# Hand order for the first stage, more staging tiles and a reordered finish in a gated MLP with a spectral branch

## Chip, cores, metric

The kernel runs on one core of a Trainium2 chip. The metric is device time in microseconds (us) of one execution; a median over several executions is given. The record sorts executions into a fast and a slow state by their time; every execution whose state is on record is fast but one of the kernel before (581.7 us, in group 4 of the experiments), which is left out of the ratios. Ratios are of one kernel's fast runs to the other's in the same rounds on the same chip, so they are not quite the ratios of the medians quoted. The kernel before had medians between 572.7 and 577.7 us in the different rounds, so differences of a per cent are judged within rounds.

## The reference

`x` is 2048 rows of 576 numbers (S = 2048, D = 576), bf16. It is normalised over its rows (LN1). One branch filters it in the frequency domain; the other is a gated MLP with a mixing over rows; silu of the second multiplies the first.

```python
xn = _layernorm(x)                                   # LN1
# branch A: spectral filter
X  = rfft2(xn);  X = X * (w_r + 1j*w_i);  s = irfft2(X)
# branch B: gated MLP
z  = gelu(xn @ w_in)                                 # 576 -> 2 * 2304
z1, z2 = z[..., :2304], layernorm(z[..., 2304:])
g  = w_sp @ z2 + b_sp[:, None]                       # 2048 x 2048 mixing of rows
b  = (z1 * g) @ w_out                                # 2304 -> 576
out = x + s * silu(b)
```

## The kernel before

All DFTs are matmuls by constant matrices. The stages on TensorE, in the names that the kernel uses, are:

- `xpose` and `p0`: for each of 16 row tiles of 128 rows, normalise, transpose (5 matmuls) and do the DFT over D (10 matmuls). The result is copied to a staging tile and stored to DRAM (`Ad`).
- `p1`: read `Ad` back by columns, first half of the DFT over S. `p2`, `p3`: second half, product with the filter, and back. `p4`, `p5`: inverse, stored to DRAM as `Yd`.
- `z2`: units of 5 matmuls (0.81 us) that make the second half of `z`. They have no part in the spectral chain, so `fill(n)` puts n of them into TensorE's program where it would otherwise wait.
- main stage: `z1`, the mixing `pg` and the last product `po`, with `p4` and `p5` in between. `outm` finishes a row tile.

The SyncE and TensorE programs are in the order of the source (`manual_schedule`); the other engines are ordered by a scheduler.

```python
    STG = [reg("STG", i * 2 * L, 2 * L) for i in range(3)]          # three staging tiles
    ...
    def p0(m):
        pa = psa.tile([P, 2, 512], F32, tag="a")
        ...                                                          # 10 matmuls
        sg = STG[m % 3].rearrange("p (c l) -> p c l", c=2)
        nc.scalar.activation(out=sg, in_=pa[:, :, 0:L], func=ACT.Identity)
        nc.gpsimd.dma_start(out=Adw[m], in_=sg)
    ...
    def p2(hh):
        ...
        for c in range(2):
            nc.vector.tensor_tensor(out=tt[:, c, :, :], in0=pa[:, :, 0:L], in1=wt[:, c, hh % 4:hh % 4 + 2, :], op=ALU.mult)
    ...
    def outm(q, i):
        m = 4 * q + i
        b = m % 2
        nc.sync.dma_start(out=XIN[b], in_=xv[:, m, :])
        nc.sync.dma_start(out=YIN[b], in_=Yd[m * P:(m + 1) * P, :])
        po = psa.tile([P, 2, 512], F32, tag="a")                     # psa has two buffers
        ...                                                          # 36 matmuls
        nc.scalar.activation(out=th, in_=po[:, :, 0:H2], func=ACT.Tanh, scale=0.5)
        nc.vector.scalar_tensor_tensor(out=g, in0=th, scalar=1.0, in1=po[:, :, 0:H2], op0=ALU.add, op1=ALU.mult)
        nc.vector.tensor_tensor(out=GO[b], in0=GO[b], in1=YIN[b], op=ALU.mult)
        nc.vector.tensor_tensor(out=GO[b], in0=GO[b], in1=XIN[b], op=ALU.add)
        nc.sync.dma_start(out=out2[m * P:(m + 1) * P, :], in_=GO[b])
    ...
            if fi == 0 and q > 0:                                    # four tiles finished at a time
                for i in range(4):
                    outm(q - 1, i)
                if q + 1 < NQ:
                    load_slab(q + 1)                                 # four transposing loads of w_sp
```

All loads, all stores of `outm` and the loads of w_in for the next stage go through the one SyncE queue, in the order of the source.

Of the kernel before, what the change touches and what calls it, by code (L numbers as in the profile page):

```python
# [15 lines left out]
P = 128  # L16
# [64 lines left out]
def kernel(  # L81
# [55 lines left out]
    TH = pers.tile([P, 2, D], F32)  # L137
    make_identity(nc, ident[:])
    eps = pers.tile([P, 1], F32)
# [12 lines left out]
    def reg(name, off, n):  # L152
        return AR[:, offs[name] + off: offs[name] + off + n]
# [11 lines left out]
    XN = [reg("XN", i * KS * P, KS * P) for i in range(3)]  # L165
    STG = [reg("STG", i * 2 * L, 2 * L) for i in range(3)]
    AIN = [reg("AIN", i * 8 * L, 8 * L) for i in range(4)]
    TT = [reg("TT", i * 4 * L, 4 * L).rearrange("p (c h l) -> p c h l", c=2, h=2) for i in range(2)]
# [10 lines left out]
    U = [RW[:, i * 512:(i + 1) * 512] for i in range(NU)]  # L179

    for i in range(3):
        nc.gpsimd.memset(XN[i][:, D:KS * P], 0.0)

    def load_x(c):
        t = AIN[c][:, 0:4 * D].rearrange("p (m d) -> p m d", m=4)
        if c == 0:
            for i in range(4):
                nc.sync.dma_start(out=t[:, i, :], in_=xv[:, i, :])
        else:
            nc.sync.dma_start(out=t, in_=xv[:, 4 * c:4 * c + 4, :])  # L190
        return t

    wv = B_w_in[0:(KS - 1) * P, :].rearrange("(k p) f -> p k f", p=P)
    XC = [load_x(0), load_x(1)]
    nc.sync.dma_start(out=CDSD, in_=cd_cdsd.ap().rearrange("p (k c l) -> p k c l", k=KS, c=2))
    XC += [load_x(2), load_x(3)]
    nc.gpsimd.memset(WIN2[KT:P, KS - 1, :], 0.0)
# [14 lines left out]
    def ln1(ms):  # L212
        n = len(ms)
        mv = small.tile([P, n, 2], F32, tag=f"mv{n}", bufs=3)
        for i, m in enumerate(ms):
            st = small.tile([P, 2, 6], F32, tag="st1", bufs=4)
            for h in range(2):
                nc.vector.bn_stats(out=st[:, h, :], in_=XC[m // 4][:, m % 4, h * H2:(h + 1) * H2])
            nc.vector.bn_aggr(out=mv[:, i, :], in_=st[:])
        if ms[0] < 4:  # L220
            rs = small.tile([P, n], F32, tag=f"rs{n}", bufs=3)
            nc.scalar.activation(out=rs[:], in_=mv[:, :, 1], func=ACT.Sqrt, bias=eps[:], scale=1.0)
            nc.vector.reciprocal(out=rs[:], in_=rs[:])
        else:
            rs = rstd_of(mv, n, f"l1{n}")
        for i, m in enumerate(ms):
            ln1_of[m] = (mv[:, i, 0:1], rs[:, i:i + 1])
# [15 lines left out]
    def p0(m):  # L243
        pa = psa.tile([P, 2, 512], F32, tag="a")
        for ks in range(KS):
            for c in range(2):
                nc.tensor.matmul(pa[:, c, 0:L], lhsT=xnT[:, m, ks, :], rhs=CDSD[:, ks, c, :],  # L247
                                 start=(ks == 0), stop=(ks == KS - 1))
        sg = STG[m % 3].rearrange("p (c l) -> p c l", c=2)
        nc.scalar.activation(out=sg, in_=pa[:, :, 0:L], func=ACT.Identity)  # L250
        nc.gpsimd.dma_start(out=Adw[m], in_=sg)
# [31 lines left out]
    def p2(hh):  # L283
        ain = AIN[(hh // 8) ^ 2].rearrange("p (h l) -> p h l", h=8)
        wt = WCH[(hh // 4) % 2]
        tt = TT[(hh // 2) % 2]
        pa = psa.tile([P, 2, 512], F32, tag="a")
        for j in range(2):
            nc.tensor.matmul(pa[:, j, 0:L], lhsT=MM[:, 0, :], rhs=ain[:, hh % 8 + j, :], start=True, stop=True)
        for c in range(2):  # L290
            nc.vector.tensor_tensor(out=tt[:, c, :, :], in0=pa[:, :, 0:L], in1=wt[:, c, hh % 4:hh % 4 + 2, :], op=ALU.mult)  # L291
        if hh % 4 == 2 and hh // 4 + 2 < 8:
            load_w(hh // 4 + 2)
# [49 lines left out]

    z2s = {}

    def z2(u):
        m, n = u // NZC, u % NZC
        on_act = m % 2 == 1 and m < MT - 2
        if n == 0:
# [10 lines left out]
        else:  # L360
            nc.scalar.activation(out=zc, in_=ph[:], func=ACT.Gelu_apprx_tanh)  # L361
            nc.vector.bn_stats(out=st[:, n, :], in_=zc)
        if n < NZC - 1:
            return
        mv = small.tile([P, 1, 2], F32, tag="mvz")
# [48 lines left out]
    def outm(q, i):  # L414
# [4 lines left out]
        po = psa.tile([P, 2, 512], F32, tag="a")  # L419
        for fi in range(FT):  # L420
            for h in range(2):
                nc.tensor.matmul(po[:, h, 0:H2], lhsT=U[(q * FT + fi) % NU][:, i * P:(i + 1) * P],  # L422
                                 rhs=WOUT[:, fi, h * H2:(h + 1) * H2], start=(fi == 0), stop=(fi == FT - 1))
        th = TH[:, b, :].rearrange("p (h d) -> p h d", h=2)
        g = GO[b].rearrange("p (h d) -> p h d", h=2)
        nc.scalar.activation(out=th, in_=po[:, :, 0:H2], func=ACT.Tanh, scale=0.5)  # L426
        nc.vector.scalar_tensor_tensor(out=g, in0=th, scalar=1.0, in1=po[:, :, 0:H2], op0=ALU.add, op1=ALU.mult)  # L427
        nc.vector.tensor_tensor(out=GO[b], in0=GO[b], in1=YIN[b], op=ALU.mult)
        nc.vector.tensor_tensor(out=GO[b], in0=GO[b], in1=XIN[b], op=ALU.add)
        nc.sync.dma_start(out=out2[m * P:(m + 1) * P, :], in_=GO[b])  # L430

# [8 lines left out]

    def fill(n):
        for u in zq:
            z2(u)
            n -= 1
            if n == 0:
                break

    with tc.manual_schedule(engines={mybir.EngineType.SP, mybir.EngineType.PE}):
        groups = [[0], [1], [2, 3], [4, 5, 6, 7], [8, 9, 10, 11], [12, 13, 14, 15]]
        nc.sync.dma_start(out=MM, in_=cd_mm.ap().rearrange("p (a k) -> p a k", a=3))  # L450
        load_w(0)
        load_w(1)
        nc.sync.dma_start(out=G4, in_=cd_g4.ap().rearrange("p (s k) -> p s k", s=N2))
        nc.sync.dma_start(out=CESO, in_=cd_ceso.ap().rearrange("p (a c l) -> p a c l", a=NLC, c=2))
        ready = 0
        for m in range(MT):
            while ready < min(m + 2, MT):
                ln1(groups[0])
                for mm in groups.pop(0):
                    ready = mm + 1  # L460
            if m == 0:
                xpose(0)
            if m + 1 < MT:
                xpose(m + 1)
            p0(m)
            if m >= 9:
                fill(2)
        for ch in range(4):
            p1_read(ch)
        fill(8)  # L470
        for s2 in range(0, N2, 2):
            p1(s2)
            fill(1)
        for ch in range(4):
            p23_read(ch)
        fill(8)
        p2(0)
# [14 lines left out]
        nc.sync.dma_start(out=BB, in_=B_b_sp.rearrange("(a s) -> a s", a=1).to_broadcast((P, S)))  # L492
        fill(MT * NZC)
        z1(0)
        au = [partial(p4, u) for u in range(4 * NLC)] + [partial(p5, j) for j in range(MT)]
# [51 lines left out]
```

## Time and profile before

| | kernel before |
|---|---|
| median, us (6 runs, before the prediction) | 577.25 |
| span of the profiled run, us | 574.5 |
| TensorE busy | 543.5 us, 95% |
| first mixing matmul (`pg`) starts at | 155.0 us |
| last matmul ends at | 568.9 us |
| last matmul to end | 5.6 us |

The page of the kernel before: the busy time of each engine (PE is TensorE, DVE VectorE, ACT ScalarE, POOL GpSimd), and the row of granted TensorE clock in 40 slices, in tenths.

```profile
PE 543.5 (95%) x3128; PEld 301.3 (52%) x3128; DVE 217.7 (38%) x424; ACT 165.6 (29%) x323; POOL 37.1 (6%) x95
...
PEclk9989799999999999999999999999999999999999
```

TensorE is the limit over the whole program; 31 us of idle are what can be had. The table by stretches of the kernel before shows where they are. Its columns are the stretch, its length, PE busy (matmuls), granted clock, DMA share and GB/s.

```profile
0.00:10.00 10.00, 1.57 (x12) 1.00 0.80 250
10.00:20.00 10.00, 9.55 (x75) 1.00 1.07 356
20.00:30.00 10.00, 5.12 (x45) 1.00 0.98 298
...
60.00:70.00 10.00, 6.65 (x33) 0.76 0.68 245
...
200.00:400.00 200.00, 198.19 (x1057) 1.00 0.39 95
...
550.00:575.00 25.00, 18.93 (x150) 0.98 0.21 61
```

Nearly all of it is in the first 140 us and at the very end; the main stage is full. The waits of TensorE in the kernel before, in us in total, times, and the longest, say what it waited for:

```profile
PE pt L238 <- DVE AR L234: 6.7, 1, 6.7
PE pa L247 <- ACT xnT L239: 6.6, 4, 3.1
PE pa L265 <- DMA AR<-Ad: 3.4, 1, 3.4
PE ph L397 <- DMA AR<-in_B_w_in_dram: 1.8, 1, 1.8
```

The first tile comes late (6.7), ScalarE's copies come late because ScalarE itself waits for stores to free its three staging tiles (6.6), and the result of the first DFT is read back late (3.4).

This is the timeline of the last four tiles in the kernel before (start, duration, engine, line; in brackets the idle time before it and what ended it), one tile and the beginning of the next:

```profile
560.83 0.76 DVE L427 SCALAR_TENSOR_TENSOR AR<-TH,po 128x576 bf16<-128x576 f32 x1 [2.67 <-ACT TH L426]
561.72 0.46 DVE L428 TENSOR_TENSOR AR<-AR 128x576 bf16<-128x576 bf16 x1
562.21 0.46 DVE L429 TENSOR_TENSOR AR<-AR 128x576 bf16<-128x576 bf16 x1
562.70 0.34 SPq L430 DMA_DIRECT2D out_dram<-AR  x1
563.13 0.38 SPq L417 DMA_DIRECT2D AR<-in_A_x_dram  x1
563.61 0.41 SPq L418 DMA_DIRECT2D AR<-Yd  x1
...
565.24 0.75 DVE L427 SCALAR_TENSOR_TENSOR AR<-TH,po 128x576 bf16<-128x576 f32 x1 [2.56 <-ACT TH L426]
566.02 0.46 DVE L428 TENSOR_TENSOR AR<-AR 128x576 bf16<-128x576 bf16 x1
```

The load of the next y (L418) is issued only after the store of this tile (L430), because both are in one queue, in order, and the store waits for VectorE. From L428 to the next L428 is a ring: 0.95 us of VectorE, 0.03, 0.91 to the issue of y, and at most 2.41 until y has landed: at most 4.30 us. (In the turn shown L428 starts right behind L427, so y was there already; the median time from issue to landing of the loads of y is 2.3 us in this profile.) TensorE needs 4.41 us per tile (17.66 us for four), so the ring had little more than 0.1 us to spare, and in one turn of the 12 VectorE did wait for y, 1.1 us. The first operation of VectorE, L427, does not need y and is outside of the ring.

### The profile page before, as it was taken

Reading aid. Unit: us, or ns where it says so; the run is one execution under the profiler, and the core shown is the slowest. Engines: PE = TensorE matmul, PEld = TensorE weight load, DVE = VectorE, ACT = ScalarE, POOL = GpSimd, SP = SyncE. Lnnn points to the kernel's source line nnn. Section 1 sums busy time; section 2 is a strip of 40 time slices with the busy share of each in tenths; the row PEclk is TensorE's granted clock in tenths of the full one; section 3 lists DMA queues with packets and bytes.
Section 4 is the critical chain, followed back from the end, with each engine's and each line's share of the span. In section 5 each row is a group of like instructions: output and inputs, shape, how many; then the busy total and the mean of one; then the engine's idle time right before and its main releaser. Section 6 shows DMA issues by size and latency. Waiting matters only on the chain.

```text
span 574.5 us, 7798 instructions
## 1 busy us (share of the span) xinstructions
PE 543.5 (95%) x3128; PEld 301.3 (52%) x3128; DVE 217.7 (38%) x424; ACT 165.6 (29%) x323; POOL 37.1 (6%) x95
## 2 busy tenths in 40 slices
PE   4689799998999999899999999999999999999996
PEld 2556465555555554347544444754444574444464
DVE  6521466885654542223322222332222232222223
ACT  3468487777633221111111111111111111111101
POOL 3423111112100000000000000000000000000000
PEclk9989799999999999999999999999999999999999
DMA  8951438779531339511651111264111122111002
GB/s 290 319 163 53 177 124 225 175 164 205 182 114 33 95 101 276 118 52 51 133 129 32 31 32 51 63 151 99 32 31 32 51 63 73 32 31 52 0 17 88
DMA packets 77380, 59.46 MB, mean 104 GB/s; under 512 B 36768, under 2 KB 71456, under 8 KB 77088
## 3 DMA queue, kind: packets, MB, share of 16 engines
q1 hardware_dynamic: 76576, 56.60, 36.5%
q0 software_dynamic: 768, 2.37, 1.3%
q8 instruction: 24, 0.39, 0.3%
q14 instruction: 12, 0.10, 0.1%
HBM read 38.74 MB, written 11.82 MB: 88 GB/s over the span
## 4 chain that ended last, share of the span: by engine, by line
PE 76%; DMA 8%; DVE 6%; SPq 4%; ACT 3%; issue 2%; POOL 1%; POOLq 0%; DVEq 0%; ACTq 0%
PE pg L408 40%; PE po L422 12%; PE ph L397 12%; PE ph L355 6%; SPq L387 3%; DMA Ad<-AR 3%; PE pa L332 2%; PE pa L247 2%; DMA AR<-in_A_w_i_dram 2%; DVE AR L291 1%; ACT TH L367 1%; DMA AR<-in_A_x_dram 1%; PE pa L315 1%; DMA AR<-Ad 1%; DMA AR<-Bd 1%
## 5 line engine op out<-in xcount | busy, mean ns | idle before, releaser
L411 DVE TENSOR_TENSOR AR<-pg,AR 128x512 bf16<-128x512 f32 x72 | 49.8, 692 | 213.3 <-PE pg L408 213.3
L399 ACT ACTIVATE AR<-ph 128x512 bf16<-128x512 f32 x72 | 43.0, 597 | 239.1 <-PE ph L397 239.0
L397 PE MATMUL ph<-xnT,AR 128*128 128x512 bf16 x360 | 89.5, 379 | 1.8 <-DMA AR<-in_B_w_in_dram 1.8
L355 PE MATMUL ph<-RW,xnT 128*128 128x384 bf16 x480 | 89.5, 331 | 0.5 <-ACT z_0_74 L361 0.5
L422 PE MATMUL po<-AR,RW 128*128 128x288 bf16 x576 | 71.2, 286 | 0.0
L422 PEld LDWEIGHTS <-RW 128*128 128x128 bf16 x576 | 56.4, 98 | 14.9
L355 PEld LDWEIGHTS <-xnT 128*128 128x128 bf16 x480 | 47.6, 99 | 29.1 <-issue 2.5
L397 PEld LDWEIGHTS <-AR 128*128 128x128 bf16 x360 | 34.9, 98 | 41.9 <-DMA AR<-in_B_w_in_dram 2.6
L247 PE MATMUL pa<-AR,xnT 128*128 128x289 bf16 x160 | 25.9, 314 | 8.3 <-ACT xnT L239 6.6
L412 DVE TENSOR_TENSOR RW<-AR 128x512 bf16<-128x512 bf16 x72 | 30.6, 425 | 7.0 <-DVE AR L411 0.5
L426 ACT ACTIVATE TH<-po 128x576 f32<-128x576 f32 x16 | 10.4, 651 | 77.6 <-PE po L422 77.6
L427 DVE SCALAR_TENSOR_TENSOR AR<-TH,po 128x576 bf16<-128x576 f32 x16 | 12.1, 754 | 47.0 <-ACT TH L426 47.0
L408 PE MATMUL pg<-AR,z_0_74 128*128 128x512 bf16 x72 | 27.3, 379 | 0.0
L408 PE MATMUL pg<-AR,z_8_82 128*128 128x512 bf16 x72 | 27.3, 379 | 0.0
L408 PE MATMUL pg<-AR,z_1_75 128*128 128x512 bf16 x72 | 27.3, 379 | 0.0
L408 PE MATMUL pg<-AR,z_2_76 128*128 128x512 bf16 x72 | 27.3, 379 | 0.0
L408 PE MATMUL pg<-AR,z_3_77 128*128 128x512 bf16 x72 | 27.3, 379 | 0.0
L408 PE MATMUL pg<-AR,z_4_78 128*128 128x512 bf16 x72 | 27.3, 379 | 0.0
L408 PE MATMUL pg<-AR,z_5_79 128*128 128x512 bf16 x72 | 27.3, 379 | 0.0
L408 PE MATMUL pg<-AR,z_6_80 128*128 128x512 bf16 x72 | 27.3, 379 | 0.0
L408 PE MATMUL pg<-AR,z_7_81 128*128 128x512 bf16 x72 | 27.3, 379 | 0.0
L408 PE MATMUL pg<-AR,z_9_83 128*128 128x512 bf16 x72 | 27.3, 379 | 0.0
(157 smaller groups left out, 676.3 us busy)
## 6 DMA issues: line engine op xcount, KB each, us to landing
AR<-in_B_w_in_dram SPq DMA_DIRECT2D x24, 384.0 KB, 3.6
AR<-in_A_x_dram SPq DMA_DIRECT2D x20, 144.0 KB, 2.3
AR<-in_B_w_out_dram SPq DMA_DIRECT2D x1, 2592.0 KB, 10.3
AR<-in_A_w_r_dram SPq DMA_DIRECT2D x16, 144.5 KB, 3.7
Ad<-AR POOLq DMA_DIRECT2D x16, 144.5 KB, 4.8
AR<-in_A_w_i_dram SPq DMA_DIRECT2D x16, 144.5 KB, 3.7
AR<-Ad SPq DMA_DIRECT2D x4, 578.0 KB, 5.8
Bd<-AR SPq DMA_DIRECT2D x4, 578.0 KB, 2.8
```

The lines of the kernel that those rows point to most:

```text
L247: nc.tensor.matmul(pa[:, c, 0:L], lhsT=xnT[:, m, ks, :], rhs=CDSD[:, ks, c, :], start=(ks == 0), stop=(ks == KS - 1))
L332: nc.tensor.matmul(pa[:, c, 0:L], lhsT=V[:, lc, c, 2 * j:2 * j + 2, :], rhs=CESO[:, lc, c, :], start=(lc == 0), stop=(lc == NLC - 1))
L355: nc.tensor.matmul(ph[:], lhsT=xnT[:, m, ks, :], rhs=WIN2[:, ks, n * ZC:(n + 1) * ZC], start=(ks == 0), stop=(ks == KS - 1))
L387: nc.sync.dma_start_transpose(out=SLAB[q % 2][:, :, i * P:(i + 1) * P], in_=wspv[t0:t0 + P, :, :])
L397: nc.tensor.matmul(ph[:].rearrange("p (a t) -> p a t", a=4), lhsT=wb[:, ks, (fi % WG) * P:(fi % WG + 1) * P], rhs=xnT[:, 4 * q:4 * q + 4, ...
L399: nc.scalar.activation(out=Z1T[k % 3], in_=ph[:], func=ACT.Gelu_apprx_tanh)
L408: nc.tensor.matmul(pg[:], lhsT=Z2[m][:, fi * P:(fi + 1) * P], rhs=SLAB[q % 2][:, m, :], start=(m == 0), stop=(m == MT - 1))
L411: nc.vector.tensor_tensor(out=tmp, in0=pg[:], in1=BB[:, q * 512:(q + 1) * 512], op=ALU.add)
L412: nc.vector.tensor_tensor(out=U[k % NU], in0=tmp, in1=Z1T[k % 3], op=ALU.mult)
L422: nc.tensor.matmul(po[:, h, 0:H2], lhsT=U[(q * FT + fi) % NU][:, i * P:(i + 1) * P], rhs=WOUT[:, fi, h * H2:(h + 1) * H2], start=(fi == 0) ...
L426: nc.scalar.activation(out=th, in_=po[:, :, 0:H2], func=ACT.Tanh, scale=0.5)
L427: nc.vector.scalar_tensor_tensor(out=g, in0=th, scalar=1.0, in1=po[:, :, 0:H2], op0=ALU.add, op1=ALU.mult)
```

## The change

The intent is to close the idle time at both ends of the program. LN1 and the D-DFT are put in hand order on VectorE too, statistics one tile at a time; eight staging tiles instead of three; DFT constants loaded right after the first row tile; 12 matmuls on zeros wake TensorE's clock; `fill` units are moved behind the loop to cover the read-back; two constant tables are loaded later; VectorE's products of `p2` get priority; the last row tile is finished by halves, and in all row tiles VectorE multiplies the PSUM result by y first and by (1 + tanh) second. Smaller edits are left out of the cut below: the identity matrix for the transposes comes by a load, ScalarE takes its Square for tile 0 instead of tile 13, a GELU is called early, and the normalisation of `z2` is issued later.

```diff
+    PST = [reg("BES", i * 2 * L, 2 * L) for i in range(8)]
...
         if c == 0:
             for i in range(4):
                 nc.sync.dma_start(out=t[:, i, :], in_=xv[:, i, :])
+                if i == 0:
+                    nc.sync.dma_start(out=CDSD, in_=...)              # constants of the D-DFT
...
-        sg = STG[m % 3].rearrange("p (c l) -> p c l", c=2)
+        sg = PST[m % 8].rearrange("p (c l) -> p c l", c=2)
...
-            nc.vector.tensor_tensor(out=tt[:, c, :, :], ...)
+            with tc.high_priority():
+                nc.vector.tensor_tensor(out=tt[:, c, :, :], ...)
...                                                                    # finish of a row tile (outm)
+        last = m == MT - 1
+        order = [(fi, h) for h in range(2) for fi in range(FT)] if last else [(fi, h) for fi in range(FT) for h in range(2)]
...
-        nc.scalar.activation(out=th, in_=po[:, :, 0:H2], func=ACT.Tanh, scale=0.5)
-        nc.vector.scalar_tensor_tensor(out=g, in0=th, scalar=1.0, in1=po[:, :, 0:H2], op0=ALU.add, op1=ALU.mult)
-        nc.vector.tensor_tensor(out=GO[b], in0=GO[b], in1=YIN[b], op=ALU.mult)
-        nc.vector.tensor_tensor(out=GO[b], in0=GO[b], in1=XIN[b], op=ALU.add)
-        nc.sync.dma_start(out=out2[m * P:(m + 1) * P, :], in_=GO[b])
+        for sl in ([slice(0, 1), slice(1, 2)] if last else [slice(0, 2)]):
+            ph = po[:, sl, 0:H2]
+            nc.scalar.activation(out=th[:, sl], in_=ph, func=ACT.Tanh, scale=0.5)
+            nc.vector.tensor_tensor(out=g[:, sl], in0=ph, in1=y[:, sl], op=ALU.mult)
+            nc.vector.scalar_tensor_tensor(out=g[:, sl], in0=th[:, sl], scalar=1.0, in1=g[:, sl], op0=ALU.add, op1=ALU.mult)
+            nc.vector.tensor_tensor(out=g[:, sl], in0=g[:, sl], in1=x[:, sl], op=ALU.add)
+            nc.sync.dma_start(out=o[:, sl], in_=g[:, sl])
...                                                                    # the program's beginning
+        for i in range(3):
+            pw = psh.tile([P, 512], F32, tag="h")
+            for j in range(4):
+                nc.tensor.matmul(pw[:], lhsT=warm[:, 0:P], rhs=warm, start=True, stop=True)
+        ln1([0])
+        xpose(0)
+        p0(0)
...                                                                    # then one tile at a time, two ahead
             if m >= 9:
-                fill(2)
+                fill(1, norm=False)
...
         for ch in range(4):
             p1_read(ch)
-        fill(8)
+        load_w(0)
+        load_w(1)
+        fill(14)
```

More of the change, by code (lines that the diff above doesn't have):

```diff
@@ L9 @@
 from concourse._compat import with_exitstack
-from concourse.masks import make_identity
 ACT = mybir.ActivationFunctionType
@@ L137 @@
     TH = pers.tile([P, 2, D], F32)
-    make_identity(nc, ident[:])
+    cd_id = nc.inline_tensor(_bf16_np(np.eye(P)), name="c_id")
+    nc.scalar.dma_start(out=ident[:], in_=cd_id.ap())
+    scr = pers.tile([P, 1], F32)
     eps = pers.tile([P, 1], F32)
@@ L179 @@
     U = [RW[:, i * 512:(i + 1) * 512] for i in range(NU)]
+    warm = Z2[MT - 1][:, 0:512]
+    nc.vector.memset(warm, 0.0)
     for i in range(3):
-        nc.gpsimd.memset(XN[i][:, D:KS * P], 0.0)
+        nc.vector.memset(XN[i][:, D:KS * P], 0.0)
     def load_x(c):
@@ L188, in load_x @@
                 nc.sync.dma_start(out=t[:, i, :], in_=xv[:, i, :])
+                if i == 0:
+                    nc.sync.dma_start(out=CDSD, in_=cd_cdsd.ap().rearrange("p (k c l) -> p k c l", k=KS, c=2))
         else:
@@ L193 @@
     wv = B_w_in[0:(KS - 1) * P, :].rearrange("(k p) f -> p k f", p=P)
-    XC = [load_x(0), load_x(1)]
-    nc.sync.dma_start(out=CDSD, in_=cd_cdsd.ap().rearrange("p (k c l) -> p k c l", k=KS, c=2))
-    XC += [load_x(2), load_x(3)]
+    XC = [load_x(c) for c in range(4)]
     nc.gpsimd.memset(WIN2[KT:P, KS - 1, :], 0.0)
@@ L219, in ln1 @@
             nc.vector.bn_aggr(out=mv[:, i, :], in_=st[:])
-        if ms[0] < 4:
+        if ms[0] < 2:
             rs = small.tile([P, n], F32, tag=f"rs{n}", bufs=3)
@@ L290, in p2 @@
         for c in range(2):
-            nc.vector.tensor_tensor(out=tt[:, c, :, :], in0=pa[:, :, 0:L], in1=wt[:, c, hh % 4:hh % 4 + 2, :], op=ALU.mult)
+            with tc.high_priority():
+                nc.vector.tensor_tensor(out=tt[:, c, :, :], in0=pa[:, :, 0:L], in1=wt[:, c, hh % 4:hh % 4 + 2, :], op=ALU.mult)
         if hh % 4 == 2 and hh // 4 + 2 < 8:
@@ L344 @@
     z2s = {}
+    pending = []
+    ACT_SUMS = (0, 1, 3, 5, 7, 9, 11)
     def z2(u):
         m, n = u // NZC, u % NZC
-        on_act = m % 2 == 1 and m < MT - 2
+        on_act = m in ACT_SUMS
         if n == 0:
@@ L362, in z2, with z2_norm @@
             nc.vector.bn_stats(out=st[:, n, :], in_=zc)
-        if n < NZC - 1:
-            return
+        if n == NZC - 1:
+            pending.append((m, st, on_act))
+    def z2_norm(m, st, on_act):
         mv = small.tile([P, 1, 2], F32, tag="mvz")
@@ L419, in outm @@
         po = psa.tile([P, 2, 512], F32, tag="a")
-        for fi in range(FT):
-            for h in range(2):
-                nc.tensor.matmul(po[:, h, 0:H2], lhsT=U[(q * FT + fi) % NU][:, i * P:(i + 1) * P],
-                                 rhs=WOUT[:, fi, h * H2:(h + 1) * H2], start=(fi == 0), stop=(fi == FT - 1))
-        th = TH[:, b, :].rearrange("p (h d) -> p h d", h=2)
-        g = GO[b].rearrange("p (h d) -> p h d", h=2)
-        nc.scalar.activation(out=th, in_=po[:, :, 0:H2], func=ACT.Tanh, scale=0.5)
-        nc.vector.scalar_tensor_tensor(out=g, in0=th, scalar=1.0, in1=po[:, :, 0:H2], op0=ALU.add, op1=ALU.mult)
-        nc.vector.tensor_tensor(out=GO[b], in0=GO[b], in1=YIN[b], op=ALU.mult)
-        nc.vector.tensor_tensor(out=GO[b], in0=GO[b], in1=XIN[b], op=ALU.add)
-        nc.sync.dma_start(out=out2[m * P:(m + 1) * P, :], in_=GO[b])
+        last = m == MT - 1
+        order = [(fi, h) for h in range(2) for fi in range(FT)] if last else [(fi, h) for fi in range(FT) for h in range(2)]
+        for fi, h in order:
+            nc.tensor.matmul(po[:, h, 0:H2], lhsT=U[(q * FT + fi) % NU][:, i * P:(i + 1) * P],
+                             rhs=WOUT[:, fi, h * H2:(h + 1) * H2], start=(fi == 0), stop=(fi == FT - 1))
+        th, g, y, x = (t.rearrange("p (h d) -> p h d", h=2) for t in (TH[:, b, :], GO[b], YIN[b], XIN[b]))
+        o = out2[m * P:(m + 1) * P, :].rearrange("p (h d) -> p h d", h=2)
+        for sl in ([slice(0, 1), slice(1, 2)] if last else [slice(0, 2)]):
[5 more added lines that the diff above has]
+            nc.sync.dma_start(out=o[:, sl], in_=g[:, sl])
     def load_win1(g):
@@ L439, with fill @@
     zq = iter(range(MT * NZC))
-    def fill(n):
+    def fill(n, norm=True):
         for u in zq:
             z2(u)
+            while norm and pending and pending[0][0] < u // NZC:
+                z2_norm(*pending.pop(0))
             n -= 1
@@ L446, in fill @@
                 break
-    with tc.manual_schedule(engines={mybir.EngineType.SP, mybir.EngineType.PE}):
-        groups = [[0], [1], [2, 3], [4, 5, 6, 7], [8, 9, 10, 11], [12, 13, 14, 15]]
-        nc.sync.dma_start(out=MM, in_=cd_mm.ap().rearrange("p (a k) -> p a k", a=3))
-        load_w(0)
-        load_w(1)
-        nc.sync.dma_start(out=G4, in_=cd_g4.ap().rearrange("p (s k) -> p s k", s=N2))
-        nc.sync.dma_start(out=CESO, in_=cd_ceso.ap().rearrange("p (a c l) -> p a c l", a=NLC, c=2))
-        ready = 0
-        for m in range(MT):
-            while ready < min(m + 2, MT):
-                ln1(groups[0])
-                for mm in groups.pop(0):
-                    ready = mm + 1
-            if m == 0:
-                xpose(0)
+    SP, PE, DVE = mybir.EngineType.SP, mybir.EngineType.PE, mybir.EngineType.DVE
+    with tc.manual_schedule(engines={SP, PE, DVE}):
+        for i in range(3):
[4 more added lines that the diff above has]
+        xpose(0)
+        nc.sync.dma_start(out=MM, in_=cd_mm.ap().rearrange("p (a k) -> p a k", a=3))
+        p0(0)
+        ln1([1])
+        xpose(1)
+        ln1([2])
+        p0(1)
+        ln1([3])
+        xpose(2)
+        for m in range(2, MT):
+            if m + 2 < MT:
+                ln1([m + 2])
             if m + 1 < MT:
@@ L465 @@
             p0(m)
+            if m == 2:
+                nc.scalar.activation(out=scr[:], in_=ln1_of[3][0], func=ACT.Gelu_apprx_tanh)
             if m >= 9:
-                fill(2)
+                fill(1, norm=False)
+    with tc.manual_schedule(engines={SP, PE}):
         for ch in range(4):
             p1_read(ch)
-        fill(8)
+        load_w(0)
+        load_w(1)
+        fill(14)
         for s2 in range(0, N2, 2):
@@ L475 @@
             p23_read(ch)
+        nc.sync.dma_start(out=G4, in_=cd_g4.ap().rearrange("p (s k) -> p s k", s=N2))
+        nc.sync.dma_start(out=CESO, in_=cd_ceso.ap().rearrange("p (a c l) -> p a c l", a=NLC, c=2))
         fill(8)
@@ L493 @@
         fill(MT * NZC)
+        while pending:
+            z2_norm(*pending.pop(0))
         z1(0)
```

## The prediction

> **What bounds the kernel now.** TensorE: the page has PE busy 543.5 of 574.5 us. In the table by stretches PE is full from 200 us on (150.0 of 150 us for 400-550), a 128x512 matmul every 0.216 us: nothing to gain there. The 31 us of idle lie at the ends: 8.4 us in the first 10, 4.9 in 20-30, 1.6 in 30-40, 3.4 in 60-70, about 4 in 90-140, 6 in the last 25. The waits of PE name them: first normalised tile 6.7, ScalarE's copy of the transposes 6.6, DFT constants 1.7, read-back of the D-DFT result 3.4. Idle also costs clock: ten D-DFT matmuls take 2.6 us at 9.7 and at 31.3 us, 1.42 warm; granted clock is 0.76 in 60-70.
>
> **Why.** ScalarE copies in order, and with three staging tiles waits 7.5 us for stores that land up to 7.6 us after issue; the transposes' copies stand behind it, so PE stops. The last D-DFT copy stands behind a 2.1 us Square, its store behind a chain on GpSimd: the read-back is issued at 62.0 us, lands at 66.4, PE has run dry.
>
> **The change, step by step.**
> 1. DFT constants load right after row tile 0, whose statistics no longer share VectorE with tiles 1-3. First D-DFT matmul at about 7.0 us instead of 9.7, at full clock thanks to 12 zero matmuls (about 5 us cold, estimate from 289 columns in 0.258 us). Tile 1 lands behind the constants (estimate 7 us): gaps until about 14 us, in which PE might cool again.
> 2. Eight staging tiles: ScalarE no longer waits for stores. Per tile PE needs 1.53 us, ScalarE 1.35, VectorE 1.38. GpSimd has 14 single powers (0.19 + 0.55) and 16 issues (0.78), about 25 us, just under PE. PE nearly continuous from 14 us, loop ending near 41.
> 3. One fill unit (0.815 us of PE) per tile in the loop and 14 after it: read-back landing about 10 us after the loop (estimate), against 11.4 us of fill. The 3.4 us wait and the cold start of p1 (2.2 us) go; p1 starts at about 53 us instead of 66.5, with one unit less done.
>    Steps 1-3: about 14.5 us, all critical, since the rest is PE-bound.
> 4. Priority for the VectorE products of p2: of about 4 us idle there, part is in-order VectorE (1.5 + 1.2), part weight loads of 5.2 us, which stay; two late constant loads compete. Gain 0.5-1 us.
> 5. Last tile by halves, product with y beside tanh: 0.65 + 0.75 + 0.46 + 0.46 us after the last matmul become about 1.2 (estimate by halving): gain 1.2.
> Square of tile 0 instead of 13, earlier GELU table load (1.28 us): neutral.
>
> **Prediction:** 577.25 - 14.5 - 0.7 - 1.2, about 561 us; range 555-567. Faster by over 2%: 0.85; within 2%: 0.14; slower: 0.01.
>
> The Trainium skill, "TensorE: Matmul & The Clock Gate", Part 1, says the array starts at half clock until about 3.4 us of activity; this trace agrees (0.258 against 0.125 us per matmul).
>
> **Right if** the profile shows D-DFT matmuls from 7 us at 0.125 us spacing, no ScalarE wait for stores, PE full from 14 us, no wait for the read-back, p1 at 52-54 us, main stage unchanged, tail 1.2 us shorter.
>
> **Wrong if** GpSimd's single powers pace the loop, PE stays at half clock through the early gaps, the read-back still comes late because a Square precedes the last copy, or late constants slow p2's weight loads.

## The result and the profile after

| | before | after |
|---|---|---|
| median, us | 577.65 (40 runs) | 571.49 (20 runs) |
| ratio of fast runs | | 0.9909, 95% interval 0.9885 to 0.9933 |
| span of the profiled run, us | 574.5 | 571.0 |
| first `pg` matmul starts at, us | 155.0 | 140.0 |
| first `pg` to last matmul, us | 413.9 | 421.9 |
| last matmul to end, us | 5.6 | 9.1 |

The change gains 0.9%, where 2.8% were predicted, and the time lies outside the range. The three lower rows split the span: 15.0 us gained before the main stage, 8.0 us lost within it, 3.5 us lost behind it. 15.0 - 8.0 - 3.5 is the 3.5 us by which the spans differ. This split is of one execution each, while the 40 executions of the kernel before lie between 571.8 and 583.0 us.

The page of the kernel after:

```profile
PE 544.5 (95%) x3140; PEld 300.3 (53%) x3140; DVE 225.2 (39%) x430; ACT 166.9 (29%) x324; POOL 43.1 (8%) x112
...
PEclk9999999999999999999999999998999999999998
```

The table by stretches of the kernel after, same stretches:

```profile
0.00:10.00 10.00, 7.43 (x32) 1.00 0.85 283
10.00:20.00 10.00, 7.97 (x75) 1.00 1.06 346
20.00:30.00 10.00, 10.00 (x95) 1.00 0.54 185
...
60.00:70.00 10.00, 9.06 (x60) 1.00 0.41 166
...
200.00:400.00 200.00, 193.18 (x1004) 0.98 0.36 90
...
550.00:575.00 25.00, 11.90 (x98) 0.86 0.21 60
```

The beginning is as intended: full from 20 us on, clock at 1.00 (the 7.43 us of the first stretch hold 5.3 us of zeros). But 200 to 400 us, which had been nearly full, now lacks 6.8 us and some clock. The waits of TensorE in the kernel after name it:

```profile
PE ph L406 <- DMA AR<-in_B_w_in_dram: 6.8, 3, 3.4
PE pa L251 <- ACT xnT L243: 1.7, 2, 0.9
```

L406 is `z1`, and what it waits for are the weights w_in. The waits on ScalarE's copies are down from 6.6 to 1.7 us and the read-back is gone from the list. What VectorE waited for has a line on the load of y (`Yd`). In the kernel before it was this:

```profile
DVE AR L428 <- DMA AR<-Yd: 1.1, 1, 1.1
```

and in the kernel after it is this:

```profile
DVE AR L439 <- DMA AR<-Yd: 41.2, 12, 3.8
```

L439 is the product with y. The timeline of the last tiles in the kernel after, same stretch of work as shown of the kernel before:

```profile
554.76 0.76 DVE L439 TENSOR_TENSOR AR<-po,AR 128x576 bf16<-128x576 f32 x1 [3.33 <-DMA AR<-Yd]
555.55 0.76 DVE L440 SCALAR_TENSOR_TENSOR AR<-TH,AR 128x576 bf16<-128x576 f32 x1
556.34 0.46 DVE L441 TENSOR_TENSOR AR<-AR 128x576 bf16<-128x576 bf16 x1
556.83 0.34 SPq L442 DMA_DIRECT2D out_dram<-AR  x1
557.26 0.38 SPq L426 DMA_DIRECT2D AR<-in_A_x_dram  x1
557.73 0.41 SPq L427 DMA_DIRECT2D AR<-Yd  x1
560.08 0.76 DVE L439 TENSOR_TENSOR AR<-po,AR 128x576 bf16<-128x576 f32 x1 [3.28 <-DMA AR<-Yd]
```

Now all three operations of VectorE are in the ring: 2.04 us, 0.03, 0.90 to the issue of y, 2.2 for y to land and 0.1 more: 5.32 us in the turn shown, 5.2 to 5.9 us in the twelve turns of the program, against TensorE's 4.41. Three such turns put the last tile 3 us late at the end of the program. In the middle, the chain that ended last in the kernel after shows what follows from it (start, us, what; SPq L442 is the last of four stores, L396 the transposing loads of w_sp):

```profile
368.65 0.77 DVE AR L439
...
370.72 0.34 SPq L442
...
371.10 1.91 SPq L396
373.06 2.19 SPq L396
375.30 3.29 SPq L396
378.63 2.40 SPq L396
381.12 4.24 DMA AR<-in_B_w_in_dram
385.41 2.32 PE ph L406 x5
387.73 4.00 PE pg L417 x16
391.72 1.08 PE ph L406 x5
```

The stores are late, the four loads behind them occupy SyncE for 9.9 us, the weights behind those come late, and TensorE, once fed, is at half clock: 2.32 us for five matmuls that take 1.08 us warm, and 4.00 for 16 that take 3.45.

**Theory A.** The product with y first, straight from PSUM, puts all of VectorE's work on a row tile behind the load of y, which stands in the SyncE queue behind the store of the tile before. All losses follow from that. Rivals: **B**, the program now is 15 us ahead of its loads (or loads were moved late), so the weights come late anyway. **C**, the finish by halves costs. **D**, VectorE's work as such is longer in the new order (0.76 + 0.76 + 0.46 against 0.75 + 0.46 + 0.46 us), not the wait.

The Trainium skill, "DMA: Bandwidth & Descriptors", section "Anatomy of one DMA — SWDGE (gpsimd) path", says that DMA engines wait on no semaphores: "any semaphore wait happens on the issuing sequencer before dispatch". The trace agrees: no load is issued between the store's wait and its issue. The same section puts the fixed cost of a DMA issued from GpSimd at about 2.0 us and the data rate at 436 GB/s, which for the 144 KB of y would be an estimate of 2.3 us; the loads of y are issued from SyncE, for which the section gives no such fit, and their median to landing here is 2.4 us.

### The profile page after: what moved, and what is told of

Same layout as the page of the kernel before. It is cut to its first block, busy times and chain, and to the rows that moved or that the text cites. A ratio compares the mean times of both kernels' runs of the same rounds, so it can differ in the third digit from the quotient of the medians.

```text
span 571.0 us, 7840 instructions
## 1 busy us (share of the span) xinstructions
PE 544.5 (95%) x3140; PEld 300.3 (53%) x3140; DVE 225.2 (39%) x430; ACT 166.9 (29%) x324; POOL 43.1 (8%) x112
## 4 chain that ended last, share of the span: by engine, by line
PE 72%; SPq 8%; DMA 8%; DVE 6%; ACT 3%; issue 2%; POOL 1%; DVEq 0%; ACTq 0%
PE pg L417 36%; PE ph L406 11%; PE ph L362 9%; SPq L396 6%; PE po L432 5%; DMA AR<-Yd 4%; PE pa L251 3%; DMA AR<-in_B_w_in_dram 2%; PE pa L337 2%; DVE AR L440 2%; DVE AR L439 2%; ACT TH L376 1%; DVE AR L441 1%; PE pb L306 1%; PE pa L320 1%
## 5 line engine op out<-in xcount | busy, mean ns | idle before, releaser
L406 PE MATMUL ph<-xnT,AR 128*128 128x512 bf16 x360 | 90.6, 383 | 6.8 <-DMA AR<-in_B_w_in_dram 6.8
L362 PE MATMUL ph<-RW,xnT 128*128 128x384 bf16 x480 | 87.1, 326 | 0.0
L406 PEld LDWEIGHTS <-AR 128*128 128x128 bf16 x360 | 35.0, 98 | 47.8 <-DMA AR<-in_B_w_in_dram 8.3
L439 DVE TENSOR_TENSOR AR<-po,AR 128x576 bf16<-128x576 f32 (+1 forms) x17 | 12.3, 722 | 56.4 <-DMA AR<-Yd 41.2
L438 ACT ACTIVATE TH<-po 128x576 f32<-128x576 f32 (+1 forms) x17 | 10.6, 623 | 81.6 <-PE po L432 74.1
L417 PE MATMUL pg<-AR,z_1_75 128*128 128x512 bf16 x72 | 27.8, 386 | 0.0
L417 PE MATMUL pg<-AR,z_0_74 128*128 128x512 bf16 x72 | 27.8, 386 | 0.0
L417 PE MATMUL pg<-AR,z_2_76 128*128 128x512 bf16 x72 | 27.7, 385 | 0.0
L417 PE MATMUL pg<-AR,z_3_77 128*128 128x512 bf16 x72 | 27.5, 383 | 0.0
L417 PE MATMUL pg<-AR,z_4_78 128*128 128x512 bf16 x72 | 27.5, 383 | 0.0
L417 PE MATMUL pg<-AR,z_5_79 128*128 128x512 bf16 x72 | 27.5, 383 | 0.0
L417 PE MATMUL pg<-AR,z_6_80 128*128 128x512 bf16 x72 | 27.5, 383 | 0.0
L417 PE MATMUL pg<-AR,z_7_81 128*128 128x512 bf16 x72 | 27.5, 382 | 0.0
L417 PE MATMUL pg<-AR,z_8_82 128*128 128x512 bf16 x72 | 27.3, 380 | 0.0
L417 PE MATMUL pg<-AR,z_9_83 128*128 128x512 bf16 x72 | 27.3, 379 | 0.0
L417 PE MATMUL pg<-AR,z_10_84 128*128 128x512 bf16 x72 | 27.3, 379 | 0.0
## 6 DMA issues: line engine op xcount, KB each, us to landing
Ad<-AR POOLq DMA_DIRECT2D x16, 144.5 KB, 3.7
AR<-in_A_w_r_dram SPq DMA_DIRECT2D x16, 144.5 KB, 5.0
AR<-in_A_w_i_dram SPq DMA_DIRECT2D x16, 144.5 KB, 4.4
```

What stands on the lines that cost most here:

```text
L362: nc.tensor.matmul(ph[:], lhsT=xnT[:, m, ks, :], rhs=WIN2[:, ks, n * ZC:(n + 1) * ZC], start=(ks == 0), stop=(ks == KS - 1))
L406: nc.tensor.matmul(ph[:].rearrange("p (a t) -> p a t", a=4), lhsT=wb[:, ks, (fi % WG) * P:(fi % WG + 1) * P], rhs=xnT[:, 4 * q:4 * q + 4, ...
L417: nc.tensor.matmul(pg[:], lhsT=Z2[m][:, fi * P:(fi + 1) * P], rhs=SLAB[q % 2][:, m, :], start=(m == 0), stop=(m == MT - 1))
L439: nc.vector.tensor_tensor(out=g[:, sl], in0=ph, in1=y[:, sl], op=ALU.mult)
```

## The experiments

Edits are against the kernel after unless said otherwise. Runs of one group shared a chip and the runs of the kernel before.

| group | run | median, us | kernel before in the same rounds | ratio (95% interval) |
|---|---|---|---|---|
| 1 | e1_tanh_first | 559.29 | 574.31 | 0.9763 (0.9696 to 0.9831) |
| 1 | e2_before_y_first | 584.03 | 574.31 | 1.0189 (1.0127 to 1.0251) |
| 1 | e3_loads_ahead | 558.98 | 574.31 | 0.9762 (0.9702 to 0.9821) |
| 1 | e4_old_finish | 558.93 | 574.31 | 0.9752 (0.9696 to 0.9807) |
| 2 | e5_no_zeros | 559.82 | 572.70 | 0.9781 (0.9749 to 0.9813) |
| 2 | e6_three_staging | 564.86 | 572.70 | 0.9859 (0.9830 to 0.9887) |
| 2 | e7_before_eight_staging | 564.61 | 572.70 | 0.9861 (0.9831 to 0.9890) |
| 2 | e8_no_priority | 562.23 | 572.70 | 0.9819 (0.9791 to 0.9846) |
| 3 | e13_tanh_first_again | 559.94 | 577.34 | 0.9706 (0.9662 to 0.9749) |
| 3 | e9_two_psum_tiles | 562.00 | 577.34 | 0.9737 (0.9690 to 0.9784) |
| 3 | e10_slabs_spread | 557.10 | 577.34 | 0.9659 (0.9614 to 0.9704) |
| 3 | e12_before_two_edits | 565.31 | 577.34 | 0.9802 (0.9758 to 0.9845) |
| 4 | e14_halves_and_loads_ahead | 556.47 | 574.99 | 0.9683 (0.9656 to 0.9710) |
| 4 | e15_same_y_first | 556.38 | 574.99 | 0.9688 (0.9658 to 0.9719) |

All results were correct.

### Group 1: where the gain went

**e1_tanh_first.** One thing undone, the order of the two products:

```diff
-            nc.vector.tensor_tensor(out=g[:, sl], in0=ph, in1=y[:, sl], op=ALU.mult)
-            nc.vector.scalar_tensor_tensor(out=g[:, sl], in0=th[:, sl], scalar=1.0, in1=g[:, sl], op0=ALU.add, op1=ALU.mult)
+            nc.vector.scalar_tensor_tensor(out=g[:, sl], in0=th[:, sl], scalar=1.0, in1=ph, op0=ALU.add, op1=ALU.mult)
+            nc.vector.tensor_tensor(out=g[:, sl], in0=g[:, sl], in1=y[:, sl], op=ALU.mult)
```

> Changed kernel with one thing undone: in the finish of every row tile (halves of the last tile kept), VectorE again takes (1+tanh) times PSUM first and the product with y second. Theory A (the y-first product waits for the load of y, which stands in the SyncE queue behind the store of the tile before; finishes fall to 5.4 us per tile, the store queue runs late, weights for the next stage come late, TensorE idles and cools): the main stage takes 414 us from first to last matmul as in the kernel before, no wait of TensorE for w_in over 1 us in the middle, time 561 us (558 to 564). Rival B (weights come late because the whole program is 15 us ahead of its loads or loads were moved late): unchanged near 571. Rival C (the finish by halves of the last tile costs): unchanged near 571.

Measured: 559.29 us, by medians 12 us less than the kernel after. The two were measured in different rounds; by their ratios to the kernel before (0.9763 and 0.9909) the difference is 8.4 us. From the first `pg` (138.8 us) to the last matmul (551.7 us) it is 412.9 us, against 421.9 in the kernel after and 413.9 in the kernel before, and from there to the end 5.7 us against 9.1 in the kernel after. TensorE's wait for w_in, in the waits of e1, is down to this:

```profile
PE ph L406 <- DMA AR<-in_B_w_in_dram: 1.3, 2, 1.0
```

Theory A stands, B and C fall: the program is just as far ahead of its loads, and the halves are still there.

**e2_before_y_first.** The counter-test, the new order alone in the kernel before:

```diff
-        nc.vector.scalar_tensor_tensor(out=g, in0=th, scalar=1.0, in1=po[:, :, 0:H2], op0=ALU.add, op1=ALU.mult)
-        nc.vector.tensor_tensor(out=GO[b], in0=GO[b], in1=YIN[b], op=ALU.mult)
+        nc.vector.tensor_tensor(out=g, in0=po[:, :, 0:H2], in1=YIN[b].rearrange("p (h d) -> p h d", h=2), op=ALU.mult)
+        nc.vector.scalar_tensor_tensor(out=g, in0=th, scalar=1.0, in1=g, op0=ALU.add, op1=ALU.mult)
```

> Kernel before with one thing added: product with y first, straight from PSUM, (1+tanh) second. Nothing else. Theory A: the loss belongs to the order alone, so it shows here too: finishes at about 5.4 us per tile, TensorE waits of 2 to 4 us for w_in after the second and third group of finishes, time 12 us over the kernel before, about 589 us (584 to 593). Rival B: no change, 577 us, because this program is not ahead of its loads.

Measured: 584.03 us, 9.7 us over the kernel before by medians (1.9% by fast runs). The waits of VectorE have the line of the kernel after again, and TensorE waits 5.9 us for w_in, three times:

```profile
DVE AR L427 <- DMA AR<-Yd: 40.8, 12, 4.4
```

The loss belongs to this one edit and needs nothing of the rest of the change. The expected size, 12 us, was a little high.

**e3_loads_ahead.** The order of products of the kernel after kept, the cause of the wait taken away:

```diff
+    def load_xy(m):
+        nc.sync.dma_start(out=XIN[m % 2], in_=xv[:, m, :])
+        nc.sync.dma_start(out=YIN[m % 2], in_=Yd[m * P:(m + 1) * P, :])
...                                                                    # in outm
-        nc.sync.dma_start(out=XIN[b], in_=xv[:, m, :])
-        nc.sync.dma_start(out=YIN[b], in_=Yd[m * P:(m + 1) * P, :])
+        if i == 0:
+            load_xy(m)
+        if i < 3:
+            load_xy(m + 1)                                             # ahead of this tile's store
```

> Changed kernel, y-first product kept, but the loads of x and y for row tile i+1 are issued in the SyncE queue before the store of row tile i (the two buffers are free by then). Theory A: the wait of VectorE for y goes from 41 us to under 2, finishes run at TensorE's 4.4 us, no wait for w_in over 1 us after them, time 560.5 us (557 to 564). Rival D (it is the longer VectorE work of the new order, 0.77 + 0.77 + 0.47 instead of 0.75 + 0.46 + 0.46 us, that matters, not the wait for the load): near 571.

Measured: 558.98 us, and no wait for y is left in VectorE's list. Its operations take as long as in the kernel after (0.76, 0.76 and 0.46 us), so D falls: it is the position of the load in the queue. What VectorE then waits for in the product with y is ScalarE's tanh, 16 times (43.5 us in sum), although that product does not use the tanh.

**e4_old_finish.** The whole finish of the kernel before (no halves, old order) in the kernel after.

> Changed kernel with the whole finish of the kernel before (no halves, old order). Theory A: 562 us (559 to 565), about 1 us over e1, which is what the halves of the last tile are worth; after the last matmul 5.6 us to the end as before, against 4.5 in e1. Rival B: near 571.

Measured: 558.93 us, no slower than e1. The expectation of 1 us for the halves was a miss. The timeline of e1 shows why: the halves did not overlap with TensorE at all.

```profile
551.70 0.41 ACT L438 ACTIVATE TH<-po 128x288 f32<-128x288 f32 x1 [3.76 <-PE po L432]
552.14 0.45 DVE L439 SCALAR_TENSOR_TENSOR AR<-TH,po 128x288 bf16<-128x288 f32 x1 [2.43 <-ACT TH L438]
552.63 0.41 ACT L438 ACTIVATE TH<-po 128x288 f32<-128x288 f32 x1 [0.52 <-DVE AR L439]
```

The first tanh starts when the last of all 36 matmuls is done, not after the first 18, and the second tanh waits for VectorE to have read the first half. VectorE's last result comes 2.9 us after the last matmul (551.7 to 554.6), in e4 2.4 us (551.7 to 554.1).

### Group 2: what the gain at the beginning is made of

The base of these is e1 (559.3 us, again 559.9 in group 3; it did not run in the rounds of group 2, so differences under 1 us are not read). Within these rounds e5, which measured the same as e1, can stand for it.

**e5_no_zeros.** The 12 matmuls on zeros taken away (the loop `for i in range(3): ... pw ...` deleted).

> Base is the run with tanh first (559.3 us). Taken away: the 12 matmuls on zeros. If they do what the prediction says, the first D-DFT matmuls come about 1.2 us earlier (transposes no longer wait behind zeros that run to 6.5 us) but at half clock, and since TensorE has gaps until 14 us the clock may stay down until 15 to 17 us: ten D-DFT matmuls in 2.6 us three or four times, time 1 to 4 us longer, 560 to 563 us. Rival: the gaps before 14 us come from the arrival of tile 1 and the powers on GpSimd, not from TensorE, so half clock hides in them: within 0.7 us of 559.3.

Measured: 559.82 us. The zeros bring nothing that these runs can show. Without them the first D-DFT matmuls start at 6.72 us (7.60 in the kernel after, 7.06 in e1), take 2.60 us for ten, and from 10.66 us on they run at full clock (1.43 us with the latency of the last). The slower first ten hide in the gaps before 14 us. The first `pg` starts at 138.9 us, in e1 at 138.8.

**e6_three_staging.** `sg = PST[m % 8]` back to `sg = STG[m % 3]`.

> Base is the run with tanh first (559.3 us). Undone: eight staging tiles back to three. If staging was the main cause of the early waits, ScalarE waits again for stores, 5 us or more in sum, and the program is 4 to 8 us longer, 563 to 567 us. Rival: the order of LN1 and the later bulk loads carry the gain, three tiles would do: within 1 us of 559.3.

Measured: 564.86 us, about 5 us more (5.0 over e5 in the same rounds). ScalarE waits 5.6 us for its stores again, TensorE 5.5 us for ScalarE's copies, and the first `pg` is at 143.2 us.

**e7_before_eight_staging.** The kernel before with the eight staging tiles alone (the same two lines).

> Kernel before with eight staging tiles alone. If staging is the main cause: the 7.5 us of ScalarE's waits for stores go, most of the 6.6 us of TensorE waiting for ScalarE's copies goes, 4 to 8 us faster, 567 to 571 us on a chip where the kernel before needs 575. Rival: the powers of four rows at a time and the read-back hold it as well; under 2 us faster.

Measured: 564.61 us against 572.70, 8.1 us faster by that edit alone. TensorE's wait for ScalarE's copies (6.6 us) is gone from its list, the wait for the first tile (6.9) is not. The two gains overlap: e6, which is e1 without the eight tiles, is 7.8 us under the same 572.70.

**e8_no_priority.** `with tc.high_priority():` taken from VectorE's products of `p2`.

> Base is the run with tanh first (559.3 us). Taken away: the priority of VectorE's products of p2. The prediction gave it (with the late loads against it) 0.5 to 1 us: 560 us. Rival, from the table of stretches of the changed kernel, which has 5.9 us of TensorE idle between 60 and 120 us against 4.2 between 70 and 140 before: the priority brings nothing, 558.5 to 559.5 us.

Measured: 562.23 us, 2 to 3 us more than e1 (2.4 over e5 in the same rounds, whose intervals just overlap). The rival's reading of the table by stretches was wrong, and the prediction's 0.5 to 1 us too small: without the priority TensorE waits 3.7 us for VectorE in `p3`, with it 1.6.

### Group 3: putting it together

**e13_tanh_first_again.** e1 again, for a comparison in the same rounds.

> The same kernel as e1_tanh_first, again, only to stand in the same rounds as the next three: 559.3 us (558 to 561).

Measured: 559.94 us.

**e12_before_two_edits.** The kernel before with eight staging tiles and the priority, nothing else.

> Kernel before with two small edits alone, eight staging tiles and the priority of VectorE's products of p2. If these two carry most of the gain and add up (8 us and 2.9 us as measured apart), 10 to 12 us faster than the kernel before, within 3 us of e1. If they overlap, no faster than the eight tiles alone, 564 us.

Measured: 565.31 us. That is 12.0 us under the kernel before by medians and 2.0% by fast runs, as expected if the two add up. But it is not within 3 us of e13 (5.4 us over it), and no faster by its median than the eight tiles alone in group 2, though by the ratios, of different rounds, 0.6% faster. So the rest of the change (one tile at a time, early constants, fill moved behind the loop; these were not tested one by one) is worth about 5 us beyond these two edits; whether the priority does anything without it is left open.

**e9_two_psum_tiles.** e1 with the two halves of the last tile in two PSUM tiles:

```diff
-        po = psa.tile([P, 2, 512], F32, tag="a")
         last = m == MT - 1
+        pos = [psa.tile([P, 2, 512], F32, tag="a", name=f"po{h}") for h in range(2 if last else 1)]
...
-            ph = po[:, sl, 0:H2]
+            ph = pos[sl.start][:, sl, 0:H2]
```

> e1_tanh_first with the two halves of the last row tile accumulated in two PSUM tiles instead of the two banks of one. In e1 the first tanh began only after the last of all 36 matmuls, and the second waited for VectorE's read of the first half: the halves ran one after the other and ended 2.9 us after the last matmul against 2.4 us for the undivided finish of e4. If the cause is that both halves are one PSUM tile to the program, the first half now ends while TensorE works on the second, the last VectorE result comes 1.3 us after the last matmul, time 1.5 us shorter than e1. Rival: the hardware or the program's order keeps them in a row whatever the tiles; unchanged.

Measured: 562.00 us, range 559.0 to 564.1 (e13: 558.8 to 562.0). The time is a miss. The mechanism worked: the first tanh starts at 554.02 us, 2.2 us before the second at 556.22. But the products with y now wait for the load of y (VectorE waits 0.32 us, and the first half's result is held until then). The profiled run lost time elsewhere, in `p2`, where VectorE waited 3.3 us for filter weights (1.2 us in e13); that stretch of the program is the same in both, and why its loads landed later is not settled.

**e10_slabs_spread.** e9, with the four transposing loads of w_sp spread: one per step behind the loads of w_in, and in `p2` not ahead of the filter weights.

```diff
-            if hh % 4 == 2 and hh >= 16:
-                load_slab(0, [hh // 4 - 4])
+            if hh % 4 == 2 and hh >= 20:
+                load_slab(0, [hh // 4 - 5] if hh < 28 else [2, 3])
...
+            if LAST < k <= LAST + 4:
+                load_slab(1, [k - LAST - 1])
+            if 1 <= fi <= 4 and 0 < q < NQ - 1:
+                load_slab(q + 1, [fi - 1])
```

> e9 with the transposing loads of w_sp spread: in p2 the first comes after the last load of A_w instead of before it, in the main stage one per step behind the loads of w_in instead of four in a row ahead of them. In e1 the chain of p2 passes through such a load and 4.9 us of A_w landing, and TensorE waits 1.3 us for w_in once. If the SyncE queue's order is the cause, 1 to 2 us faster than e9: 556 to 557 us. Rival: the landing time of A_w itself is the limit, not the queue: within 0.5 us of e9.

Measured: 557.10 us, the narrowest range of its group (556.8 to 557.9). It is 4.9 us under e9, more than expected, but e9 was itself slower than its base, and 2.8 us under e13. The wait for w_in is gone from TensorE's list and that for filter weights from VectorE's. For w_in the order of the SyncE queue is thereby shown to be the cause; for the filter weights it is likely and not shown, as e1's profile had no such wait either and e13's had 1.2 us.

### Group 4: the step of the prediction that had appeared in no run

**e14_halves_and_loads_ahead.** e10 with the loads of x and y ahead, as in e3.

> e10 (557.1 us) with the loads of x and y of a tile issued ahead of the store of the tile before. If only the queue kept the halves from working, no wait for y is left, the first half's store is issued while TensorE works on the second half, VectorE's last result comes 1.3 us after the last matmul (undivided finish: 2.4, e10: 1.8), 0.5 to 1 us faster than e10, 556.3 us. Rival: end of the program is set by the landing of the last store, whatever comes before; unchanged.

Measured: 556.47 us, the fastest together with e15. The timeline of the end:

```profile
548.01 0.41 ACT L444 ACTIVATE TH<-po 128x288 f32<-128x288 f32 x1 [1.55 <-PE po L438]
...
550.21 0.41 ACT L444 ACTIVATE TH<-po 128x288 f32<-128x288 f32 x1 [1.79 <-PE po L438]
550.65 0.45 DVE L445 SCALAR_TENSOR_TENSOR AR<-TH,po 128x288 bf16<-128x288 f32 x1 [1.07 <-ACT TH L444]
551.14 0.31 DVE L446 TENSOR_TENSOR AR<-AR 128x288 bf16<-128x288 bf16 x1
551.48 0.31 DVE L447 TENSOR_TENSOR AR<-AR 128x288 bf16<-128x288 bf16 x1
```

VectorE is done 1.6 us after the last matmul (550.2 to 551.8), and the program ends 4.3 us after it (span 554.5), in e4 5.5 us. (In e10 VectorE took 2.3 us, 549.7 to 552.0, not the 1.8 of the expectation.) The end is thus 1.2 us shorter, as in the prediction's last step, but only when each half has its own PSUM tile and y is there in time; of this VectorE's part is 0.8 us (2.4 to 1.6).

**e15_same_y_first.** e14 with the product by y first.

> e14 with the product by y first. With the load early, y first can run beside tanh of the last half, so the end is 0 to 0.3 us earlier than e14, and the extra 0.3 us of VectorE per tile hide under TensorE: within 0.5 us of e14. If y first is harmful as such: 3 us or more longer.

Measured: 556.38 us, the same as e14. The order of the products is indifferent once the load of y is early; it was never harmful as arithmetic. Nor did it ever gain what it was made for: the product with y does not run beside tanh. For 16 of the 17 such products (the last tile has two) VectorE waits until ScalarE's tanh of the same PSUM tile is done:

```profile
DVE AR L445 <- ACT TH L444: 42.6, 16, 3.9
```

The two operations share only the PSUM tile that both read. Whether the program or the hardware keeps them in a row was not tested.

## Why the prediction was wrong, point by point

- **Steps 1 to 4, the beginning: right in sum.** The prediction had 14.5 + 0.7 us; the first `pg` starts 15.0 us earlier. The loop ends at 40.2 us (41 predicted), `p1` starts at 52.5 (53), no wait for the read-back is left, TensorE is full from about 14 us. The sum is in part luck: the terms do not add (e6, e7), the zeros gave nothing (e5) and step 4 was worth more than predicted (e8).
- **Step 1: the zeros were credited wrongly.** The first D-DFT matmuls came at 7.6 us (7.1 in e1), not 7.0, because the transposes stood behind the zeros; without zeros there is no loss (e5). Within 0 to 14 us the arrival of tiles, not TensorE's clock, sets the pace.
- **Step 2: right, and the largest term tested alone**: 8.1 us on the kernel before (e7), 5 us when taken back (e6). GpSimd's single powers did not pace the loop: TensorE is busy 10.00 of 10 us from 20 to 30 us.
- **Step 4: the sign was right, the size off.** 0.5 to 1 us net were predicted; taking the priority away costs 2 to 3 us (e8).
- **Step 5 is the step that failed.** As put: "Last tile by halves, product with y beside tanh: ... gain 1.2." It treated the new order of products as a matter of the last tile. The edit applies to all 16 tiles, and it moves the first need of y from VectorE's second operation to its first. The ring of store, load of y, products grew from at most 4.30 us to 5.32 (5.2 to 5.9) per tile, over TensorE's 4.41. That was in reach of the trace of before: its durations and its queue order give both numbers. In place of a gain of 1.2 us the finish cost 9 to 12 us (571.5 against 558.9 in e4, which is of other rounds; by the ratios to the kernel before 9.0 us; in the same rounds, e2 against the kernel before, 9.7 us): in the profiled run 8.0 us within the main stage, by late weights and a cold clock, and 3.5 us behind it. The overlaps that step 5 counted on failed too. The halves ran in a row, since both were one PSUM tile (e4, e9); with that and the queue mended the end is 1.2 us shorter (e14). And the product with y never ran beside tanh: it waited for tanh wherever y was there in time (4 of 16 tiles in the kernel after, 16 of 17 products in e3 and e15).
- Had step 5 been costed zero, the prediction would have been 562 us; e4, which is that kernel, measures 558.9.

On the clock: the Trainium skill, "TensorE: Matmul & The Clock Gate", Part 1, says that an idle window of about 3.4 us puts TensorE back to half clock. The main stage agrees in kind: after the gap before 385.41 us in the chain shown, five matmuls take 2.32 us against 1.08 and the next sixteen 4.00 against 3.45. The gap was 2.6 us (17.4 of the 20 us from 370 to 390 are busy), which is shorter than the page's window, so a wait of 2.6 us cost 4.4 us. The same skill's rule in "DMA: Bandwidth & Descriptors", "Rules for kernel authors", is to issue a DMA early and wait on its semaphore late; e3 follows that rule for the loads of x and y and changes nothing else, which is worth 8 to 12 us here (by ratios and by medians).

## What to carry to other kernels

When operands of a chain are swapped, ask for each which wait it brings to the front of the chain, in every iteration and not only where the gain is sought: a load that was hidden behind one operation may be in the ring once it is needed first. Compare the length of each such ring (store, next load in the same queue, landing, work up to the next store) with the time of the engine that should set the pace; here at most 4.30 us and 5.32 us stood on the two sides of 4.41. In a queue that is served in order, put loads for the next iteration ahead of the store of this one, and long issues behind what is needed sooner.

## What the Trainium skill lacked or had wrong

- "TensorE: Matmul & The Clock Gate", Part 1, ties the return to half clock to an idle window of about 3.4 us. In the main stage of the kernel after a gap of 2.6 us was enough (382.8 to 385.4 us; the matmuls behind it are 0.43 us apart instead of 0.216). Behind a gap of 3.4 us (278.4 to 281.8) five matmuls still ran at full clock before the next eight were at half. In the profile of e3 TensorE fell back at about 14.5 us (ten matmuls in 2.03 and 2.23 us, 1.42 before and after) although none of its gaps between 6.8 and 14.5 us was longer than 1.0 us; it had been busy 2.9 and 2.7 us of the two stretches of 5 us before. The other runs with the same beginning did not fall back. The page mentions frequent short idles as a cause but gives no figure for how sparse the activity must be.
- The same page advises to warm up before a benchmark with 4 us of matmuls or more. In a kernel whose first stage waits for its data anyhow, 4.4 to 5.3 us of zeros brought nothing that the runs can show (559.8 us without, 559.3 and 559.9 with), and held the first transposes back (they start at 5.2 us without, at 5.4 to 6.3 with). This is no error of the page, which speaks of benchmarks.
- "DMA: Bandwidth & Descriptors" gives no time for which a transposing load of this size holds its issuing queue on this chip. Here each holds SyncE for 1.9 to 8.8 us (kernel after, median 2.6, for 128 rows of w_sp), four in a row for 9.9 us in the chain shown, 16.1 us at 199 us, and all later loads of the queue wait.
- The formula of the same page for DMAs issued from GpSimd, 2.0 us plus bytes over 436 GB/s, came close for y (2.3 us estimated, 2.4 measured), though y is loaded from SyncE. It was far off for stores that GpSimd issues in the first 30 us, when the DMA engines were all but fully busy: for their 144.5 KB it gives an estimate of 2.3 us, and in the kernel before they took up to 7.6 us.
